# Sinkhorn attention and a token-mixing MLP on one core: a rewritten second half of the hand-written order, wider weights for turning k', and a last output row in two halves

## The chip, the cores and the metric

The kernel runs on one core of a Trainium2 chip. The time is device microseconds of one execution; the figure quoted is the median of several runs. One of the executions was also recorded by the hardware profiler, and all rows below come from that recording.

## What is computed

Four batches, eight heads, 768 positions, head size 64. The reference first turns an 8 by 8 matrix per head into a nearly doubly stochastic P by five rounds of exp and normalisation, mixes the eight blocks of 96 positions of k and v with it, attends within each block, and passes the result x (768 by 512 per batch) through a mixer over positions:

```python
k_sorted = np.einsum('bhij,bhjcd->bhicd', P, k_b)        # v_sorted likewise
scores = scale * np.matmul(q_b, k_sb.transpose(0, 1, 2, 4, 3))
attn = exp(scores - max) / sum;  x = attn @ v_sb
wq = x @ w_q;  wk = x @ w_k
mixed = (wq @ wk.T / 8) @ x
out = np.maximum(mixed, 0.0) @ w_out
```

The first half is written per head, the mixer per batch. The kernel computes mixed as wq times (wk.T x), so that no 768 by 768 matrix is made.

## The kernel before

All work is cut into units with short names, and one string, `ORDER` (from line 20), lists them in program order; line 661 walks through it. A unit's name is a letter, the batch and a number: `P23` is product group 3 of batch 2. Capital letters are TensorE units that write PSUM, and the number behind the colon is the first of the 512-column PSUM banks (0 to 7) that they write; the same letter in lower case is the unit that empties the banks, with its engine (A ScalarE, D VectorE, G GpSimd, S SyncE). A TensorE unit therefore waits until whoever used its banks last has emptied them. Each engine works through its own units in the order of the string, so the string decides both the sequence on every engine and which unit waits for which.

The units, batch by batch (a batch has `b`, the line is that of the function):

- `l`: loads of q, k, v by GpSimd's queue (line 220); `p`, `Q`/`q`: q is rearranged by a copy and turned by TensorE (262, 271, 274), two heads at a time.
- `K`/`k` and `V`/`v`: sorted k (turned, two heads at a time, 289) and sorted v (310); `R`: six DMAs per batch that bring sorted v from `Vs` into blocks, `VT` (329). `K`, `V`, `S`, `P`, `H` write two banks.
- `S`/`e`: seven groups of scores, emptied by ScalarE with exp into `E` (352, 361).
- `P`/`r`, `x`: five groups of products with v; VectorE takes the reciprocal of the sums and multiplies, into `X` (372, 385, 389). Group 4 is the small one.
- `T`/`t` (batches 0 and 1, TensorE) or `D` (batches 2 and 3, two transposing DMAs on SyncE's queue, 397): `X` is turned into `XT`. `D20` needs product groups 0 to 2 of batch 2, `D21` groups 2 to 4.
- `J`/`j`: wq and wk of one half of the positions each, turned, into `qkT` (408); `d` copies the wq part to the other 64 partitions, `qD`. `J` needs all of `XT`, so both transposing DMAs.
- `W`/`w`: wk (the change calls it k') is turned back by TensorE with `qkT` as the weights (423). `G`/`g`: wk.T x, into `Ab` (433). `H`/`h`: mixed, turned, with relu, into `mixT` (448, 456), three units per batch, each for two of the six output rows that a partition holds.
- `O`/`o`: output row n of a batch, four matmuls of 512 columns, copied to one of four buffers `ot` (469, 478). Two rows share a buffer; `s` sends them out by the queue of the engine named (482). For the last batch each row is sent by itself. A number of two digits behind the batch, as in `O323`, means a half row (`osplit`): half 2 of row 3.
- `Z`: dummy matmuls at the start, while the inputs arrive.

The buffer of rows n, n+1 of batch b is number (3b + n/2) modulo 4, so rows 2 and 3 of batch 2 (sent by `s21`) lie in the buffer that rows 4 and 5 of batch 3 (`o34`, `o35`) take over. Behind the last unit GpSimd checks all reciprocals (`guard`) and, if one isn't finite, recomputes everything in another way; with these inputs it does not.

The loop that walks the string:

```python
    for item in ORDER.split():
        kind, arg = item[0], item.split(":")[1:]
        ...
        if kind.isupper() and kind not in "RNDI":
            fns[kind](b, n, int(arg[0]))
        else:
            fns[kind](b, n, arg[0], int(arg[1]) if len(arg) > 1 else None)
```

Of the kernel before, what the change touches and what calls it, by code (L numbers as in the profile page):

```python
# [19 lines left out]
ORDER = """  # L20
i00:G i02:D I00:S A00:0 Z04:1 Z15:1 Z25:1 lv0b I01:S lk0a c00:D a01:A i03:G c01:D lv0a a02:A:0 lk0b
c02:D z11:A lv1b lv1a a03:A Q01:0 Z33:1 c03:D lk1a lq1b lk1b z10:A a04:A c04:D z12:A Q00:2 Z43:1
q01:D:0 a05:A z13:A c05:D q00:A:2 Z54:1 Q03:0 Z62:1 q03:D:0 B00:2 Q02:3 n01:D:2 n00:D:2 n03:D:2
u00:A:2 K01:4 K00:0 q02:D:3 n11:G n10:G k01:A:4 Y03:6 k00:D:0 y03:A:6 S02:4 n02:D:2 e02:A:4 Y00:0
K02:2 Y02:6 y00:A:0 k02:D:2 Y01:4 y02:A:6 S00:0 y01:D:4 lp K03:2 e00:A:0 S01:6 k03:D:2 F00:4 lq1a
e01:A:6 F01:5 f00:D:4 S06:2 S05:0 e06:A:2 f01:D:5 P00:6 e05:A:0 S03:2 r00:D:6 x00:D:6 V12:4 e03:A:2
P01:0 r01:D:0 x01:D:0 v12:A:4 S04:6 F03:2 F02:3 e04:A:6 R15:S V11:4 f02:D:3 V10:0 v11:A:4 f03:D:2
P02:6 p12:G v10:A:0 r02:D:6 x02:D:6 R12:S p13:G P04:2 R14:S K11:4 n20:G T00:0 r04:D:2 x04:D:2
k11:A:4 R13:S Q12:1 P03:6 R11:S t00:A:0 q12:D:1 lk2a K13:2 r03:D:6 x03:D:6 R10:S Q13:1 k13:A:2 lv2b
K12:4 U00:0 k12:A:4 lv2a K10:2 z01:D:0 T03:6 q13:D:1 k10:A:2 T02:7 t03:D:6 U01:4 p11:G T01:5 t02:D:7  # L30
z02:A:4 S16:2 S14:0 t01:D:5 lo e16:A:2 S15:6 Q11:4 e15:A:6 p10:G J01:5 q11:D:4 J00:2 e14:A:0 n21:G
S13:6 j00:D:2 j01:A:5 Q10:0 e13:A:6 W01:1 lq2a W00:1 P14:2 P13:4 w00:A:1 d01:G r14:D:2 x14:D:2
q10:A:0 K20:6 lq2b G00:1 r13:D:4 x13:D:4 k20:A:6 lq3a S11:2 G01:1 e11:A:2 d00:G K21:6 g00:D:1 S10:4
lk2b k21:D:6 H01:0 e10:A:4 h01:D:0 V20:2 V21:4 v20:A:2 V22:6 v21:D:4 P10:0 v22:A:6 R21:S T13:2
r10:D:0 x10:D:0 R20:S H02:4 S12:6 O02:3 R25:S e12:A:6 h02:D:4 R23:S H00:0 o02:A:3 P12:6 R22:S
h00:A:0 O03:3 p21:G r12:D:6 x12:D:6 R24:S t13:A:2 P11:4 lk3a O04:0 r11:D:4 x11:D:4 p20:G O00:2
o04:A:0 lv3a p23:A T10:0 o00:D:2 lv3b Q21:1 p22:A Q20:4 q21:D:1 T11:2 n31:G q20:A:4 T12:5 t11:D:2
O05:1 t12:A:5 o03:D:3 lq3b t10:D:0 S22:6 S20:4 e22:A:6 S21:2 lk3b o05:D:1 J11:0 p30:G e21:A:2 Q23:1
j11:D:0 J10:6 p31:G q23:D:1 e20:A:4 Q22:7 j10:D:6 W11:1 n30:G Q30:0 q22:A:7 K22:4 q30:D:0 K23:2
k22:A:4 Q31:0 s01:G k23:D:2 W10:1 P21:6 d10:G w10:A:1 d11:D S23:4 q31:D:0 S24:2 e23:A:4 O01:1  # L40
r21:D:6 x21:D:6 e24:A:2 S25:4 G10:0 o01:D:1 e25:A:4 K31:6 K30:2 k31:D:6 G11:0 k30:A:2 P22:4 g10:D:0
S26:2 r22:D:4 x22:D:4 V30:0 e26:A:2 P23:6 v30:A:0 H10:2 r23:D:6 x23:D:6 V31:4 h10:A:2 R30:S p33:G
S31:0 R31:S v31:D:4 e31:A:0 p32:G V32:6 H12:2 v32:A:6 S32:0 h12:D:2 R33:S Q33:4 Q32:5 e32:A:0 R32:S
K32:6 q33:D:4 R34:S P24:2 k32:A:6 K33:0 r24:D:2 x24:D:2 R35:S k33:A:0 P20:6 q32:D:5 D21:S H11:2
S35:0 r20:D:6 x20:D:6 h11:A:2 O14:5 e35:A:0 S33:2 o14:D:5 D20:S S36:6 O13:4 e33:A:2 P31:0 s00:S
e36:A:6 S34:2 r31:D:0 x31:D:0 P34:6 e34:A:2 O10:5 r34:D:6 x34:D:6 P32:2 o10:A:5 S30:0 r32:D:2
x32:D:2 P33:6 e30:A:0 J20:5 J21:0 r33:D:6 x33:D:6 j20:A:5 P30:2 d20:G j21:A:0 W20:5 r30:D:2 x30:D:2
d21:G W21:5 D31:S O12:6 w20:A:5 G21:5 o13:D:4 D30:S G20:5 o12:D:6 O11:4 g20:D:5 s11:S H20:6 s02:S
H22:2 h20:A:6 H21:0 h22:D:2 O15:5 o11:A:4 O21:6 o15:D:5 h21:A:0 s10:G O20:7 J30:0 J31:1 j30:D:0
O25:5 d30:G j31:D:1 d31:S W30:4 o20:D:7 W31:4 O22:1 w30:A:4 w31:A:4 o25:D:5 o21:A:6 G31:0 s12:A  # L50
G30:0 s20:A O23:6 o22:A:1 g30:A:0 H30:0 o23:D:6 H31:4 h30:A:0 H32:2 h31:D:4 O24:7 s21:S h32:A:2
O31:6 o24:A:7 O32:2 o31:D:6 s22:S O34:3 s31:A o32:D:2 O35:6 s32:A o34:A:3 O30:7 o35:D:6 s34:S O33:3
s35:A o30:D:7 s30:S o33:A:3 s33:S
"""


# [652 lines left out]
```

## Time and profile before

| | |
|---|---|
| median of 3 runs | 98.72 us (98.5 to 98.78) |
| the profiled execution's own time | 98.33 us |
| its span in the profile | 96.4 us |
| busy: TensorE / weight loads | 86.3 us (90%) / 58.7 us (61%) |
| busy: VectorE / ScalarE / GpSimd | 72.6 / 68.8 / 43.1 us |
| granted clock of TensorE | 0.991 of full speed over the span |
| DMA | 21.44 MB, 222 GB/s over the span |

The span runs from the first to the last recorded event; the execution's own time is 1.93 us longer. Busy times are sums over instructions, so an engine that is 90% busy over the span can be idle in one stretch and never idle in another; a busy TensorE need not be at its peak, because matmuls overlap and their ends are modelled. In the rows, PE is TensorE, PEld its weight loads, DVE VectorE, ACT ScalarE, POOL GpSimd and SP SyncE. "<-" at the end of a row names what ended the idle time before it.

### The profile page before, as it was taken

The numbers are of one execution on the slowest core, as the hardware profiler recorded it, in microseconds if no ns is written. First come the engines' busy times: TensorE is split into PE (matmuls) and PEld (weight loads), VectorE is DVE, ScalarE is ACT, GpSimd is POOL, SyncE is SP. The second block draws the span as 40 slices with busy tenths as digits, with TensorE's granted clock in tenths as the row PEclk, the third lists the DMA queues.
The fourth block names the chain that finished last, engine by engine and source line by source line (L and its number), as shares of the span: only waits on it lengthen the run. The fifth ranks groups of instructions, "written<-read, shape, count | busy, mean of one in ns | idle before, by whom it ended". The sixth has DMA issues, their size and how long they took to land.

```text
span 96.4 us, 3206 instructions
## 1 busy us (share of the span) xinstructions
PE 86.3 (90%) x1333; PEld 58.7 (61%) x1342; DVE 72.6 (75%) x141; ACT 68.8 (71%) x96; POOL 43.1 (45%) x70
## 2 busy tenths in 40 slices
PE   4999587999899999999999999899969999999930
PEld 2344177788787687845778687674756545644400
DVE  2767896988999469999877999987796773645520
ACT  5177629998979999796989888999746090466220
POOL 6996309700999993049998006000004021950000
PEclk9999999999999999999999999999999999999996
DMA  0899999999999999999999999379953899785992
GB/s 10 266 353 227 203 203 203 203 203 207 195 275 216 209 203 207 202 204 249 250 225 204 202 204 289 124 208 206 205 206 70 199 118 413 289 352 221 396 366 112
DMA packets 24655, 21.44 MB, mean 222 GB/s; under 512 B 7296, under 2 KB 22720, under 8 KB 24640
## 3 DMA queue, kind: packets, MB, share of 16 engines
q0 software_dynamic: 12720, 10.36, 65.5%
q1 hardware_dynamic: 11200, 9.05, 35.5%
q10 hardware_dynamic: 720, 1.84, 4.8%
q8 instruction: 10, 0.16, 0.7%
q14 instruction: 5, 0.04, 0.1%
HBM read 20.19 MB, written 6.29 MB: 275 GB/s over the span
## 4 chain that ended last, share of the span: by engine, by line
PE 55%; DVE 16%; ACT 12%; DMA 10%; issue 3%; SPq 0%; DVEq 0%; ACTq 0%
PE ps L154 55%; DMA XT<-X 5%; DMA XT<-in_q_dram 5%; DVE X L392 4%; ACT E L363 4%; ACT KT L158 3%; DVE QT L162 2%; ACT Vs L158 2%; DVE VT L162 1%; DVE Vs L162 1%; DVE M L253 1%; DVE XT L162 1%; ACT mixT L460 1%; ACT Qn L158 1%; DVE tmp L193 1%
## 5 line engine op out<-in xcount | busy, mean ns | idle before, releaser
L363 ACT ACTIVATE E<-ps 96x960 bf16<-96x960 f32 (+1 forms) x28 | 24.3, 905 | 2.2 <-PE ps L154 1.6
L154 PE MATMUL ps<-wo,mixT 128*128 128x512 bf16 x88 | 22.8, 380 | 0.4
L392 DVE TENSOR_TENSOR X<-ps,Rall 96x896 bf16<-96x896 f32 (+1 forms) x20 | 20.1, 1006 | 0.7
L160 POOL COPY Qn<-Qn 128x768 bf16<-128x768 bf16 x10 | 8.1, 831 | 16.9 <-DMA Qn<-in_q_dram 16.9
L162 DVE COPY ot<-ps 128x512 f32<-128x512 f32 (+1 forms) x16 | 10.8, 687 | 4.8 <-PE ps L154 4.5
L154 PEld LDWEIGHTS <-mixT 128*128 128x128 bf16 x96 | 8.3, 98 | 9.1 <-issue 0.8
L154 PE MATMUL ps<-VT,E 96*128 96x65 bf16 x256 | 11.2, 193 | 0.3
L154 PEld LDWEIGHTS <-KT 64*128 64x128 bf16 (+1 forms) x288 | 8.4, 97 | 4.5 <-issue 2.2
L154 PEld LDWEIGHTS <-E 96*128 96x128 bf16 x256 | 9.7, 97 | 2.1 <-issue 0.4
L158 ACT CAST KT<-ps 128x768 bf16<-128x768 f32 x13 | 10.2, 808 | 0.9 <-DVE Rall L387 0.4
L154 PE MATMUL ps<-QT,KT 64*128 64x96 bf16 x256 | 9.3, 204 | 1.1 <-ACT KT L158 0.8
L160 POOL COPY qD<-qkT 64x384 bf16<-64x384 bf16 x6 | 3.0, 505 | 15.0 <-ACT qkT L158 12.8
L460 ACT ACTIVATE mixT<-ps 128x1024 bf16<-128x1024 f32 x7 | 7.1, 1027 | 3.5 <-PE ps L154 3.5
L253 POOL TENSOR_TENSOR M<-PTR,m_p 128x512 bf16<-128x512 bf16 x6 | 7.9, 1318 | 3.6 <-ACT PTR L158 3.5
L158 ACT COPY ot<-ps 128x512 f32<-128x512 f32 x9 | 5.3, 587 | 5.1 <-PE ps L154 4.7
L154 PE MATMUL ps<-idb,Qn 128*128 128x128 bf16 x96 | 7.7, 220 | 1.1 <-DVE Pm L190 1.0
L154 PE MATMUL ps<-fil 128*128 128x512 bf16 x25 | 8.2, 482 | 0.1
L154 PE MATMUL ps<-M,Kn 128*64 128x128 bf16 x192 | 7.8, 221 | 0.1
L162 DVE CAST KT<-ps 128x768 bf16<-128x768 f32 x7 | 6.7, 955 | 1.2 <-PE ps L154 1.1
L154 PEld LDWEIGHTS <-Qn 128*128 128x128 bf16 x96 | 5.7, 98 | 3.0 <-ACT Qn L158 2.1
L158 ACT CAST Vs<-ps 128x1024 bf16<-128x1024 f32 x7 | 7.0, 1012 | 0.6 <-PE ps L154 0.5
L387 DVE RECIPROCAL Rall<-ps 96x14 f32<-96x14 f32 (+1 forms) x20 | 4.6, 228 | 3.5 <-PE ps L154 2.2
(84 smaller groups left out, 142.9 us busy)
## 6 DMA issues: line engine op xcount, KB each, us to landing
Vn<-in_v_dram POOLq DMA_DIRECT2D x8, 384.0 KB, 9.6
Kn<-in_k_dram POOLq DMA_DIRECT2D x8, 384.0 KB, 11.4
out_dram<-ot SPq DMA_DIRECT2D x5, 512.0 KB, 4.7
VT<-Vs SPq DMA_DIRECT2D x18, 132.0 KB, 5.0
Qn<-in_q_dram POOLq DMA_DIRECT2D x6, 384.0 KB, 11.4
XT<-in_q_dram SPq DMA_DIRECT2D x2, 768.0 KB, 5.7
out_dram<-ot POOLq DMA_DIRECT2D x2, 512.0 KB, 7.4
out_dram<-ot ACTq DMA_DIRECT2D x2, 512.0 KB, 2.8
```

The lines of the kernel that those rows point to most:

```text
L154: nc.tensor.matmul(o, w, x, is_transpose=t, start=start, stop=stop, skip_group_check=True)
L158: nc.scalar.copy(o, i)
L160: nc.gpsimd.tensor_copy(o, i)
L162: nc.vector.tensor_copy(o, i)
L193: nc.vector.reduce_sum(tmp, (Pm if n == 1 else Pv).rearrange("p i j -> p j i"), axis=AX.X)
L253: ENG[e].tensor_tensor(out=M[b % 2][:, h0:h0 + hn], in0=src.unsqueeze(2).to_broadcast([P, hn, SP, NB]), in1=m_p.unsqueeze(1).unsqueeze(3). ...
L363: nc.scalar.activation(E[b % 2][:, n, 0:2 * w * BLK].rearrange("p (t a c) -> p a t c", a=2, c=BLK), PS[0:BLK, bank:bank + 2, 0:w * BLK].re ...
L387: nc.vector.reciprocal(Rall[:, b, n, :, 0:w], avps(bank, w)[:, :, :, D])
L392: nc.vector.tensor_mul(xo.rearrange("p (a t d) -> p a t d", a=2, d=D), avps(bank, w)[:, :, :, 0:D], Rall[:, b, n, :, 0:w].unsqueeze(3).to_ ...
L460: nc.scalar.activation(o, i, ACT.Relu)
```

## The change

From the loads of the last batch on, the units stand in another order: from about 48 us of the span to its end. What was done before by the other engine of the pair is marked by the letter. Of the units that empty banks or copy, `j10`, `d11`, `k31`, `g10`, `h12`, `d20`, `o13`, `h22`, `j30`, `o23`, `o35` go to ScalarE, and `q22`, `w10`, `k33`, `h10`, `o11`, `h21`, `d31`, `w30`, `o21`, `o22`, `o24` to VectorE; `d30` goes to SyncE. Of the output DMAs `s01`, `s22`, `s34` go to ScalarE's queue, `s12`, `s32`, `s35` to SyncE's, `s20` and `s21` to GpSimd's. Row 3 of the last batch is computed, copied and sent in two halves of 256 columns. In the first half of the string TensorE, ScalarE and VectorE keep their sequences, but many units use other banks, so that some wait for another unit to empty theirs: `S13` now follows `S14` in its banks and no longer `S15`.

The end of the table, and the one function that changes:

```diff
-O31:6 o24:A:7 O32:2 o31:D:6 s22:S O34:3 s31:A o32:D:2 O35:6 s32:A o34:A:3 O30:7 o35:D:6 s34:S O33:3
-s35:A o30:D:7 s30:S o33:A:3 s33:S
+O31:2 o24:D:3 O30:0 s22:A o31:D:2 O32:1 s31:A o30:D:0 O35:2 s30:S o32:D:1 O34:3 s32:S o35:A:2 s35:S
+O323:2 o34:A:3 O313:1 o323:D:2 s34:A o313:D:1 s323:A s313:A
```
```diff
     def u_W(b, n, bank):
         for i in range(4 * n, 4 * n + 4):
-            mm(PS[0:BLK, bank, i * DH:(i + 1) * DH], qkT[b % 2][:, i * BLK:(i + 1) * BLK], idb[:, DH:P])
+            w = BLK if i % 4 == 3 else P
+            mm(PS[0:w, bank, i * DH:(i + 1) * DH], qkT[b % 2][:, i * BLK:i * BLK + w], idb[:, DH:P])
```

So three of four weight loads of `W` take 128 columns (the block's 96 and 32 of the next), and 128 rows of PSUM are written, of which 96 are read; in the fourth they stay 96.

On TensorE, between the units that both versions share, the order from the last `W` of batch 1 to the first `J` of batch 2 is, before:

```
W11 Q30 K22 K23 Q31 W10 P21 S23 S24 O01 S25 G10 K31 K30 G11 P22 S26 V30 P23 H10 V31 S31 V32 H12 S32
Q33 Q32 K32 P24 K33 P20 H11 S35 O14 S33 S36 O13 P31 S34 P34 O10 P32 S30 P33 J20 J21
```

and now:

```
W11 K23 K22 W10 Q30 Q31 S25 S24 O01 P20 S23 G11 K31 G10 P21 S26 V30 V31 V32 P24 H11 P22 K30 H12 P23
S31 Q33 Q32 K32 K33 S32 O14 S36 S35 H10 S34 O15 P34 S33 P33 O10 P32 S30 P31 J21 J20
```

Both hold the same kinds and numbers of units (`O15` for `O13`, `P31` for `P33` before the `J`).

The first place where instructions move is VectorE's row of units around the products of batch 2 (`X0`; `Rall` takes the reciprocals, `Vs0` is sorted v of batch 3, `QT1` and `KT1` are its q and k, `mixT1` the mixer of batch 1). Before, from the reciprocals of `P22` on:

```order
L387 RECIPROCAL Rall_109<-ps_66 96x14
L392 TENSOR_TENSOR X0_89<-ps_66,Rall_109 96x896
L387 RECIPROCAL Rall_109<-ps_66 96x14
L392 TENSOR_TENSOR X0_89<-ps_66,Rall_109 96x896
L162 CAST Vs0_84<-ps_66 128x8x2x64
L462 TENSOR_SCALAR mixT1_102<-ps_66 128x4x256
L162 COPY QT1_81<-ps_66 128x768
L387 RECIPROCAL Rall_109<-ps_66 96x2x4
L392 TENSOR_TENSOR X0_89<-ps_66,Rall_109 96x512
L162 COPY QT1_81<-ps_66 128x768
L387 RECIPROCAL Rall_109<-ps_66 96x14
L392 TENSOR_TENSOR X0_89<-ps_66,Rall_109 96x896
```

Now, from the eviction of `V31` on:

```order
L162 CAST Vs0_84<-ps_66 128x8x2x64
L387 RECIPROCAL Rall_109<-ps_66 96x2x4
L392 TENSOR_TENSOR X0_89<-ps_66,Rall_109 96x512
L387 RECIPROCAL Rall_109<-ps_66 96x14
L392 TENSOR_TENSOR X0_89<-ps_66,Rall_109 96x896
L387 RECIPROCAL Rall_109<-ps_66 96x14
L392 TENSOR_TENSOR X0_89<-ps_66,Rall_109 96x896
L162 COPY QT1_81<-ps_66 128x768
L162 CAST KT1_83<-ps_66 128x768
L162 COPY QT1_81<-ps_66 128x768
L463 TENSOR_SCALAR mixT1_102<-ps_66 128x4x256
```

The last three product groups of batch 2 (groups 4, 2, 3) now follow one another, and both copies of q and one of k of batch 3 stand behind them instead of between and before.

The second place is the end of ScalarE's row, from the copy of a row of the last batch on (`ot` are the output buffers). Before:

```order
L158 COPY ot0_103<-ps_66 128x512
L488 DMA out_0_dram<-ot1_104 128x512
L488 DMA out_0_dram<-ot2_105 128x512
L158 COPY ot3_106<-ps_66 128x512
L488 DMA out_0_dram<-ot3_106 128x512
L158 COPY ot2_105<-ps_66 128x512
```

Now:

```order
L486 DMA out_0_dram<-ot0_103 128x1024
L489 DMA out_0_dram<-ot1_104 128x512
L158 COPY ot3_106<-ps_66 128x512 x2
L489 DMA out_0_dram<-ot3_106 128x512
L489 DMA out_0_dram<-ot2_105 128x256 x2
```

The last copy of a whole row has left ScalarE, and its queue ends with three DMAs, of rows 4 and of the two halves of row 3; the halves are copied by VectorE, as its last two copies.

The third place is GpSimd's row between the copies of q of batch 3 (`Qn2`) and its check of the reciprocals (`s1`). Before:

```order
L160 COPY Qn2_71<-Qn1_70 128x2x6x64 x2
L160 COPY qD0_95<-qkT0_93 64x384 x2
L485 DMA out_0_dram<-ot3_106 128x1024
L160 COPY qD1_96<-qkT1_94 64x384
L500 TENSOR_REDUCE s1_1795<-Rall_109 1x1
```

Now:

```order
L160 COPY qD0_95<-qkT0_93 64x384
L486 DMA out_0_dram<-ot3_106 128x1024
L486 DMA out_0_dram<-ot2_105 128x1024
L486 DMA out_0_dram<-ot3_106 128x1024
L501 TENSOR_REDUCE s1_1801<-Rall_109 1x1
```

Two copies for batches 2 and 3 have left GpSimd, and two output DMAs of batch 2, `s20` and `s21`, have come to it; the check stands behind them.

## Rows read from the trace of the kernel before

**Rows 1.** Busy time by stretch; columns: stretch, length, engines with instructions, clock, DMA.
```profile
core 0: us, PE busy (x) PEld busy (x) DVE busy (x) ACT busy (x) POOL busy (x), PEclk, DMA share, GB/s
51.26:71.57 20.31, 18.99 (x382) 14.12 (x383) 17.84 (x30) 18.00 (x23) 3.00 (x5) 1.00 1.09 203
71.57:92.50 20.93, 20.77 (x159) 10.82 (x162) 12.92 (x19) 8.97 (x15) 5.29 (x11) 1.00 0.83 264
```

**Rows 2.** Chain that ended last, in order of time: start, length, what (us).
```profile
66.33 5.19 DMA XT<-X
...
92.54 0.59 ACT ot L158
```

**Rows 3.** Timeline, TensorE: start, us, instructions merged, and the idle time before them.
```profile
60.54 0.61 PE L154 MATMUL ps<-Vn,M 128*128 128x128 bf16 x8 [0.35 <-DVE X L392]
...
61.45 0.39 PE L154 MATMUL ps<-QT,KT 64*128 64x96 bf16 x10
...
61.77 0.84 PE L154 MATMUL ps<-idb,Qn 128*128 128x128 bf16 x12
...
62.54 0.53 PE L154 MATMUL ps<-M,Kn 128*64 128x128 bf16 x12
...
63.00 0.42 PE L154 MATMUL ps<-VT,E 96*128 96x65 bf16 x8
...
71.57 1.47 PE L154 MATMUL ps<-XT,wqk 128*128 128x384 bf16 x8 [0.68 <-DMA XT<-X]
...
85.53 0.28 PE L154 MATMUL ps<-qkT,Ab 64*128 64x256 bf16 x1
...
86.29 6.22 PE L154 MATMUL ps<-wo,mixT 128*128 128x512 bf16 x27
```

**Rows 4.** Groups of instructions by form: busy us, mean ns of one, idle before.
```profile
L363 ACT ACTIVATE E<-ps 96x960 bf16<-96x960 f32 x24 | 22.5, 974 | 1.9 <-PE ps L154 1.3 <-DVE XT L162 0.2 <-DVE X L392 0.2
L392 DVE TENSOR_TENSOR X<-ps,Rall 96x896 bf16<-96x896 f32 x16 | 17.4, 1087 | 0.6
...
L162 DVE COPY ot<-ps 128x512 f32<-128x512 f32 x15 | 10.1, 686 | 4.8 <-PE ps L154 4.5 <-DMA out_dram<-ot 0.2
L154 PEld LDWEIGHTS <-E 96*128 96x128 bf16 x256 | 9.7, 97 | 2.1 <-issue 0.4 <-ACT E L363 0.2
...
L158 ACT COPY ot<-ps 128x512 f32<-128x512 f32 x9 | 5.3, 587 | 5.1 <-PE ps L154 4.7 <-ACT ot L158 0.5
...
L387 DVE RECIPROCAL Rall<-ps 96x14 f32<-96x14 f32 x16 | 3.8, 236 | 2.6 <-PE ps L154 1.3 <-ACT E L363 1.2
...
L162 DVE CAST Vs<-ps 128x1024 bf16<-128x1024 f32 x2 | 2.4, 1213 | 0.0
...
L154 PEld LDWEIGHTS <-qkT 128*96 128x96 bf16 x32 | 2.0, 124 | 0.3
...
L446 DVE TENSOR_SCALAR Ab<-ps 128x256 bf16<-128x256 f32 x3 | 1.3, 417 | 0.1
```

**Rows 5.** Timeline, DMA issues on the queues of SyncE and ScalarE: start, us, issue.
```profile
64.58 1.65 SPq L398 DMA_TRANSPOSE XT<-X  x1
...
66.33 1.57 SPq L398 DMA_TRANSPOSE XT<-X  x1
...
91.54 0.34 ACTq L488 DMA_DIRECT2D out_dram<-ot  x1
```

**Rows 6.** DMA issues of single short windows: size, then median us from issue to landing.
```profile
Qn<-in_q_dram POOLq DMA_DIRECT2D x1, 384.0 KB, 11.4
...
out_dram<-ot POOLq DMA_DIRECT2D x1, 512.0 KB, 10.1
...
out_dram<-ot POOLq DMA_DIRECT2D x1, 512.0 KB, 4.6
...
qD<-qkT SPq DMA_DIRECT2D x1, 48.0 KB, 1.8
...
out_dram<-ot SPq DMA_DIRECT2D x1, 256.0 KB, 2.2
```

More of the change, by code (lines that the diff above doesn't have):

```diff
@@ L20 @@
 ORDER = """
[L21 to L49, printed above, removed]
@@ L50 @@
-O25:5 d30:G j31:D:1 d31:S W30:4 o20:D:7 W31:4 O22:1 w30:A:4 w31:A:4 o25:D:5 o21:A:6 G31:0 s12:A
-G30:0 s20:A O23:6 o22:A:1 g30:A:0 H30:0 o23:D:6 H31:4 h30:A:0 H32:2 h31:D:4 O24:7 s21:S h32:A:2
-O31:6 o24:A:7 O32:2 o31:D:6 s22:S O34:3 s31:A o32:D:2 O35:6 s32:A o34:A:3 O30:7 o35:D:6 s34:S O33:3
-s35:A o30:D:7 s30:S o33:A:3 s33:S
+i00:G i02:D I00:S lv0b A00:0 I01:S Z04:1 lk0a c00:D a01:A i03:G c01:D Z15:2 lv0a a02:A:0 lk0b c02:D
+lv1b z11:A Z25:0 lv1a a03:A c03:D lk1a z10:A Q01:2 lq1b Z33:3 a04:A c04:D Q00:0 Z43:3 z12:A lk1b
@@ new lines @@
+q01:D:2 a05:A z13:A Z54:1 c05:D q00:A:0 Q03:2 Z62:3 q03:D:2 B00:3 Q02:0 n01:D:3 n00:D:3 K01:4
+n03:D:3 K00:6 q02:D:0 u00:A:3 k01:A:4 n11:G k00:D:6 Y03:0 y03:A:0 S02:4 n02:D:3 Y00:6 n10:G K02:2
+e02:A:4 Y02:0 k02:D:2 y00:A:6 Y01:4 lp S00:2 y01:D:4 y02:A:0 K03:6 e00:A:2 lq1a k03:D:6 S01:0 F00:4
+e01:A:0 F01:5 f00:D:4 S06:6 S05:2 f01:D:5 e06:A:6 P00:0 e05:A:2 S03:6 r00:D:0 x00:D:0 V12:4 e03:A:6
+P01:2 r01:D:2 x01:D:2 v12:A:4 S04:0 F03:6 F02:7 e04:A:0 R15:S V11:4 f02:D:7 V10:2 v11:A:4 p12:G
+f03:D:6 P02:0 p13:G P04:6 v10:A:2 r02:D:0 x02:D:0 R12:S K11:4 n20:G R14:S k11:A:4 T00:2 r04:D:6
@@ new lines @@
+x04:D:6 R13:S Q12:3 t00:A:2 P03:4 lk2a R11:S q12:D:3 K13:6 r03:D:4 x03:D:4 R10:S Q13:3 lv2b k13:A:6
+K12:0 U00:2 lv2a k12:A:0 K10:6 z01:D:2 T03:4 q13:D:3 k10:A:6 T02:5 p11:G t03:D:4 U01:0 T01:1 t02:D:5
+z02:A:0 S16:6 lo S14:2 t01:D:1 e16:A:6 S15:4 e15:A:4 p10:G Q11:0 J01:1 q11:D:0 n21:G e14:A:2 J00:4
+j01:A:1 S13:2 j00:D:4 lq2a Q10:1 e13:A:2 W01:0 W00:0 d01:G P14:4 P13:6 w00:A:0 r14:D:4 x14:D:4 lq2b
+K20:2 q10:A:1 G00:0 lq3a r13:D:6 x13:D:6 k20:A:2 S11:4 d00:G G01:0 e11:A:4 K21:2 lk2b g00:D:0 S10:6
@@ new lines @@
+k21:D:2 H01:0 e10:A:6 V20:4 h01:D:0 V21:2 v20:A:4 V22:6 v21:D:2 v22:A:6 P10:0 R21:S T13:4 R20:S
+r10:D:0 x10:D:0 H02:6 S12:2 R25:S O02:5 e12:A:2 R23:S h02:D:6 H00:0 o02:A:5 R22:S P12:2 p21:G
+h00:A:0 O03:5 R24:S r12:D:2 x12:D:2 lk3a t13:A:4 P11:6 O04:0 p20:G r11:D:6 x11:D:6 O00:4 lv3a
+o04:A:0 p23:A lv3b T10:0 o00:D:4 Q21:1 p22:A Q20:6 n31:G q21:D:1 T11:4 q20:A:6 T12:7 t11:D:4 O05:1
+t12:A:7 o03:D:5 lq3b t10:D:0 S22:2 lk3b S20:6 e22:A:2 S21:4 o05:D:1 J11:0 p30:G e21:A:4 Q23:1
+j11:D:0 J10:2 n30:G q23:D:1 e20:A:6 Q22:3 W11:1 q22:D:3 K23:4 p31:G j10:A:2 K22:6 k23:D:4 W10:1
@@ new lines @@
+k22:A:6 Q30:0 d10:G Q31:2 q30:D:0 d11:A S25:4 S24:6 w10:D:1 s01:A O01:3 e25:A:4 q31:D:2 P20:0
+e24:A:6 S23:4 r20:D:0 x20:D:0 G11:2 e23:A:4 K31:6 G10:2 o01:D:3 k31:A:6 P21:4 g10:A:2 S26:0 r21:D:4
+x21:D:4 V30:6 e26:A:0 V31:2 v30:A:6 V32:0 v31:D:2 P24:4 v32:A:0 R31:S H11:6 r24:D:4 x24:D:4 R30:S
+P22:2 h11:A:6 R33:S K30:0 p33:G r22:D:2 x22:D:2 H12:4 k30:A:0 R35:S P23:6 p32:G h12:A:4 R32:S S31:0
+r23:D:6 x23:D:6 Q33:2 R34:S Q32:3 e31:A:0 K32:4 D20:S q33:D:2 K33:6 k32:A:4 S32:0 k33:D:6 O14:2
+e32:A:0 D21:S q32:D:3 S36:6 S35:4 e36:A:6 H10:0 e35:A:4 s00:S h10:D:0 S34:6 s02:S O15:3 e34:A:6
@@ new lines @@
+o14:D:2 P34:0 S33:4 r34:D:0 x34:D:0 P33:6 e33:A:4 O10:2 r33:D:6 x33:D:6 P32:4 o10:A:2 S30:0 r32:D:4
+x32:D:4 P31:6 e30:A:0 J21:2 r31:D:6 x31:D:6 J20:0 D31:S j21:A:2 P30:4 d21:G j20:A:0 W21:2 r30:D:4
+x30:D:4 W20:2 O11:0 w20:A:2 d20:A G20:2 o15:D:3 D30:S G21:2 o11:D:0 O12:3 g20:D:2 s10:G H20:0
+o12:D:3 H21:4 h20:A:0 H22:6 h21:D:4 O13:2 O21:3 o13:A:2 h22:A:6 s11:S O20:2 o21:D:3 s12:S J31:4
+o20:D:2 J30:5 j31:D:4 s20:G O22:2 d31:D j30:A:5 d30:S W31:3 W30:3 O23:5 w31:A:3 w30:D:3 o22:D:2
+G31:4 G30:4 O25:2 g30:A:4 o23:A:5 H30:6 s21:G o25:D:2 H31:4 h30:A:6 H32:0 h31:D:4 O24:3 h32:A:0
```

## The prediction, made blind

> **What bounds the kernel now.** I read four views in turn. First the busy time by stretch [rows 1], cut where TensorE ends `W11` (51.26 us), where it starts `J20` (71.57), and where its last matmul ends (92.50). The reader is to see two kinds of stretch. From 71.57 on TensorE is busy for 20.77 of 20.93 us: nothing but its own work sets the time. From 51.26 to 71.57 it is busy for 18.99 of 20.31, so 1.32 us are idle, while ScalarE (18.00) and VectorE (17.84) are nearly as full as TensorE: here three engines hold each other up. The granted clock is full in both, so no term below is about the clock. Next the chain that ended last [rows 2]: it passes through a transposing DMA of 5.19 us, issued at 66.33, and ends in ScalarE's copy of the last output row, 0.59 us. Then TensorE's timeline [rows 3], for the places of the idle time: `J20` starts 0.68 us late, waiting for that DMA, and `V32` 0.35 us late, waiting for VectorE's product `x23`. These two are 1.03 of the 1.32 us. The views of prices and DMAs [rows 4 to 6] are used below.
>
> So the change can gain in the middle stretch, at most 1.32 us unless it shortens TensorE's work, and behind the last matmul; from `J` on only by fewer nanoseconds per matmul.
>
> **The wait for the transposing DMAs.** Before, the last product group of batch 2 ahead of its transposing DMAs is `P20`; between it and `J20` TensorE has thirteen units. In the new order it is `P23`, and the same kinds of thirteen units stand behind it plus six: `S31`, `Q33`, `Q32`, `K32`, `K33`, `S32`. A group of scores takes 61.77 - 61.45 = 0.32 us, the two `Q` 62.54 - 61.77 = 0.77, a `K` 63.00 - 62.54 = 0.46 [rows 3], so the six take 2 x 0.32 + 0.77 + 2 x 0.46 = 2.33 us. Against it: before, the two DMAs were issued 66.33 - 64.58 = 1.75 us apart and the first, `D21`, was out long before `x20` ended [rows 5]. Now `x22` and `x23` follow each other on VectorE, 0.236 + 1.087 = 1.32 us apart [rows 4], while SyncE needs 1.65 us to issue a transposing DMA [rows 5]; the second goes out 0.33 us later than its data allow. The DMA is covered by 2.33 - 0.33 - 0.68 = 1.32 us more than it needs. The wait goes, **-0.68 us**, as long as the six `R` transfers, ahead of `D20` on SyncE's queue, are out by then; they follow `V30`, `V31`, `V32`, which now stand together and ahead of `P24`, so I expect them earlier than before. If that cover is gone, each microsecond by which the `R` are late is one that `J21` is late.
>
> **What is late next.** ScalarE and VectorE swap units in this stretch. By kinds the exchange is nearly even (`j10`, `k31`, `g10`, `h12` against `q22`, `k33`, `w10`, `h10`; besides, ScalarE takes a small copy and one DMA issue of 0.34 us [rows 5]). So ScalarE holds some 18.3 us and VectorE 17.8 in a stretch that would be 19.6 us without the wait: there is room, but little. The 0.35 us of `V32` go too: its banks now follow `e26`, which is short and early. A new wait comes: `P22` takes the banks of `V31`, whose eviction (1.21 us) stands on VectorE behind `x21` (0.24 + 1.09) [rows 4], so TensorE stands at `P22` for a few tenths. I put it at 0.33, about one wait like `V32`'s. Ends for the whole stretch: 0, where every wait comes back in another place, and -1.32, where TensorE never stands. Sum: -0.68 - 0.35 + 0.33 = **-0.70 us**.
>
> **The first half.** `S13` has the banks of `S14` and no longer those of `S15`. Since `e14` is ScalarE's next eviction after `e15`, `S13` may wait up to one eviction longer, 0.97 us [rows 4]; ends 0 and +0.97. TensorE has had two units between, and the units that follow wait less for ScalarE, so I take the value nearer to nothing: **+0.10**.
>
> **Weights of 128 columns.** A load of 96 columns takes 124 ns, one of 128 columns 97 [rows 4]. So 27 ns per load is the most that can come out of it, and nothing the least, as loads overlap matmuls; I take half, 13 ns. Of the 24 changed loads 12 lie behind `J21`, where TensorE is the bound: 12 x 13 ns = **-0.15 us**; the others lie beside evictions and count nothing (if TensorE were the bound there too, as much again). The Trainium skill (TensorE: Matmul & The Clock Gate, section "LDWEIGHTS (loading the stationary operand)") speaks against this edit: a load takes its columns divided by 1.2 in nanoseconds, 80 for 96 columns and 107 for 128. By that rule the term would be +0.3 and the sum below -0.65. The rows above show the wider load as the quicker one, so here the measurement decides; the same page's section on Fast Weight Load, by which 128 weights of two bytes take a faster path, agrees with them.
>
> **The end.** The last copy was 0.587 us for 512 columns on ScalarE; now it is 256 columns on VectorE: between half of 0.686 and the 0.417 of `Ab` of that size [rows 4], 0.39, so -0.20. The last transfer had 256 KB and landed in 2.2 us; one of 48 KB took 1.8 [rows 6]; for 128 KB I take 1.95, between, so -0.25. On ScalarE's queue the last DMA stands behind two more issues of 0.34 [rows 5]: `o34` ends 0.6 us after `O34`, then two issues, 1.28; the second half's copy ends 0.9 (a row's matmuls) + 0.4 = 1.3 after `O34`. So the queue costs 0.05 at most. Eight matmuls of 256 columns instead of four of 512 cost four more weight loads beside them: 0 to 4 x 0.097; I take 0.05. Sum **-0.35** (ends -0.6 and 0).
>
> **Edits that I cost at nothing.** `d30` by SyncE takes 1.8 us [rows 6] instead of a copy, but lies beside `O22`, `W`, `O23`, `G` and `O25`, some 4 us; without that cover it would cost about 1.3. `d11` and `d20` on ScalarE lie beside `G`. On SyncE's queue `s02` stands ahead of `D31`, and `s11` and `s12` ahead of `d30`; all wait for rows copied by then. GpSimd's check starts behind `s21`, yet GpSimd is busy for only 5.29 us of the last 20.93 [rows 1] and stays clear of the end.
>
> **The sum.** -0.70 + 0.10 - 0.15 - 0.35 = **-1.10 us**. The profiled execution took 98.33 us, which becomes 97.23. It lies 0.39 below the median of the runs; I take the difference over to the median: 98.72 - 1.10 = **97.62**, say 97.6 us.
>
> **Rivals.**
>
> - *The evictions are the bound.* If ScalarE and VectorE, not the DMA, hold the middle stretch, the waits come back in front of other units and only the end is gained: 0 + 0.10 - 0.15 - 0.35 = -0.40, **98.3 us**. For it: 18.00 and 17.84 of 20.31 us. Against it: both still have 2.3 us of idle time there.
> - *The last loads come late.* `s01`, 512 KB, was queued on GpSimd's queue behind the loads of batch 3 and so took 10.1 us [rows 6]. On ScalarE's queue it competes with them. At 203 GB/s [rows 1] it pushes them back by at most 2.6 us; q's last load then lands up to 14 us after its issue instead of 11.4 [rows 6], and `Q33` and `K32` stand. Most of that is slack (`Q33` ran some 3 us after that load landed); I give it 0.6 us: **98.2 us**.
> - *`s21` by GpSimd comes too late.* `o35` overwrites the buffer that `s21` reads. `s21` is issued behind `o23`, about when `H30` starts; `o35` follows three `H` (86.29 - 85.53 = 0.76) and five rows of 6.22 / 7 = 0.89 [rows 3], 5.2 us later. On GpSimd's queue such a transfer took 4.6 us in one place and 10.1 in another [rows 6]. Beyond 5.2 us each microsecond is added at the end; beyond 6.3 the change is slower. At 10.1 it would be -1.10 + 4.9 = +3.8, **102.5 us**. Against it: the 10.1 lay behind loads, and here there are none.
> - *The middle stretch loses all its idle time* (-1.32) and the end gives its best (-0.6): with the other terms -2.0, **96.7 us**.
>
> **How the numbers follow.** The forecast, from -0.5 to -1.6 us, has a chance of 0.58; the evictions 0.15, the loads 0.08, `s21` 0.07, the best case 0.12. A difference of 0.3% is 0.30 us, about what a measurement of this kernel can tell from none. Faster by more than that are the forecast, the best case, and the larger part of the two small gains: 0.80. Within it falls the rest of those two: 0.12. Slower: `s21`, and a little for the first half at its dear end: 0.08. The range reaches from the best case to the small gains and a little beyond: 96.7 to 98.6; outside lie `s21` and the tails.
>
> **What would show it.** Right: `J21` starts within a tenth of `P31`'s end and no wait for XT<-X stands before it; it begins near 70.9 us; from it to the last matmul some 20.8 us; the last copy takes 0.4, its transfer 1.9 to 2.0. Wrong: idle time of TensorE in front of `P22`, `K33` or `P34` that adds up to a microsecond; a wait of a copy of q for its load near 60 us; a copy into `ot` waiting for out_dram<-ot near 89 us; or a first half in which `W11` ends later than 51.5 us.

## The result, and the profile after

The changed kernel took 99.36 us (median; 99.12 to 100.04), the kernel before, run beside it, 98.44. The ratio is 1.0109, with a 95% interval of 1.0075 to 1.0143: **1.1% slower**. It leaves out one slow run of the kernel before, of 99.93 us, which the median includes. The forecast was 97.6 us and faster, the range ended at 98.6, and slower had a chance of 0.08. The profiled execution took 99.33 us, its span 97.5 (98.33 and 96.4 before).

The same views as before, cut at the same units: end of `W11`, start of the first `J`, last matmul. First the busy time by stretch of the changed kernel.

```profile
core 0: us, PE busy (x) PEld busy (x) DVE busy (x) ACT busy (x) POOL busy (x), PEclk, DMA share, GB/s
51.31:70.39 19.08, 18.24 (x379) 14.03 (x381) 17.08 (x28) 17.26 (x24) 2.34 (x4) 1.00 1.10 201
70.39:91.70 21.31, 21.00 (x169) 10.94 (x168) 14.82 (x24) 10.04 (x16) 5.44 (x11) 1.00 0.89 276
91.70:97.50 5.80, 0.00 (x0) 0.00 (x0) 0.39 (x2) 0.00 (x0) 0.00 (x0) 0.75 0.33 120
```

Beside [rows 1]: `W11` ends at 51.31 us (51.26 before), the middle stretch lasts 19.08 us (20.31), and the last matmul ends at 91.70 (92.50). TensorE is done 0.80 us *earlier*, and the span ends 1.1 us *later*. So all of the loss, 1.9 us, lies behind the last matmul: that piece was 3.9 us (92.50 to 96.4) and is 5.8 now, and the engines' columns show almost nothing in it. Next VectorE's last copies, ScalarE's last three DMA issues, and the third of them by itself.

```profile
91.30 0.79 DVE L162 COPY ot<-ps 128x256 f32<-128x256 f32 x2 [1.56 <-PE ps L154]
91.39 1.45 ACTq L489 DMA_DIRECT2D out_dram<-ot  x3
92.43 0.42 ACTq L489 DMA_DIRECT2D out_dram<-ot  x1
```

```profile
out_dram<-ot ACTq DMA_DIRECT2D x2, 128.0 KB, 2.1
```

The last output transfer (third row of the first fence: the issue; the second fence is the median time to landing of the two halves, of which the last took 2.0) went out at 92.43 us and landed at 94.4. Before, the last issue began near 93.15 and landed 2.2 us later, at 95.4, a microsecond ahead of the end of the span [rows 6]. The output is complete 0.9 us sooner than before, and the program still ends 1.1 us later. What ends last isn't the output. In the changed kernel the chain that ended last stops at VectorE's copy:

```profile
81.01 5.20 PE ps L154 x49
86.26 4.95 PE ps L154 x24
91.30 0.79 DVE ot L162 x2
```

That is 92.09 us, and 5.4 us of the span stand behind it without a link. The waits of SyncE's queue put a name on its last stand, and a wrong one:

```profile
SPq L705 <- DMA Vn<-in_v_dram: 3.4, 1, 3.4
SPq L705 <- PEq L705: 2.4, 2, 1.9
```

(Columns: the waiting line, what released it, us in total, times, longest. L705 is the end of the program.) A load of v, landed some 40 us earlier, can't have been what SyncE waited for. In the kernel before the same stand reads so:

```profile
SPq L704 <- DMA out_dram<-ot: 1.3, 3, 0.6
```

What does end last shows among the instructions that don't count as busy. Here is GpSimd in the changed kernel, from its last output DMA on, with the first and last of the seven instructions of `guard`, the check of the reciprocals; then, by line, its instructions at the branch (L676) and at the program's end (L705: count, shortest, median and longest in ns, first and last start in us).

```profile
84.92 0.53 POOL L486 DMA_DIRECT2D out_dram<-ot  x1 [4.09 <-ACT ot L158]
85.51 0.76 POOL L501 CROSS_LANE_REDUCE s<-Rall 96x1 f32<-96x280 f32 x1
...
89.05 0.18 POOL L507 TENSOR_SCALAR flag<-s 1x1 int32<-1x1 f32 x1
```

```profile
L676 POOLq EVENT_SEMAPHORE  x5: 17/43/43, 93.2 to 93.5; - x5
L676 POOLq COMPARE_BRANCH  x1: 45/45/45, 90.0 to 90.0; - x1
L676 POOLq INC_SWDGE_SEM  x1: 756/756/756, 93.6 to 93.6; - x1
L705 POOLq EVENT_SEMAPHORE  x4: 17/17/17, 96.8 to 97.4; - x4
L705 POOLq DRAIN  x3: 46/101/2355, 94.4 to 97.3; - x3
```

And the same of the kernel before:

```profile
82.24 0.76 POOL L500 CROSS_LANE_REDUCE s<-Rall 96x1 f32<-96x280 f32 x1
...
85.78 0.18 POOL L506 TENSOR_SCALAR flag<-s 1x1 int32<-1x1 f32 x1
```

```profile
L675 POOLq COMPARE_BRANCH  x1: 45/45/45, 86.6 to 86.6; - x1
L675 POOLq INC_SWDGE_SEM  x1: 736/736/736, 90.6 to 90.6; - x1
L704 POOLq DRAIN  x3: 46/101/2273, 91.4 to 96.1; - x3
```

Follow the times in the changed kernel: check 85.51 to 89.23, branch at 90.0, next instruction at 93.2, `INC_SWDGE_SEM` 93.6 to 94.4, `DRAIN` 94.4 to 96.75, the meeting of the engines, end of the span at 97.5. If nothing in this chain waits for another engine before that meeting, the check's start alone sets its end; from there to the end of the span it takes **12.0 us**. Before, the check started at 82.24 and the long `DRAIN` ended at 91.4 + 2.27 = 93.7. With the 0.75 us that follow it in the changed kernel the chain alone would have ended at 94.4, and the output's last landing set the end, at 96.4: 2.0 us of slack. Now the check starts behind `s21` on GpSimd's queue. `s21` waits for the copy of its row (4.09 us of standing, `<-ACT ot`), and the check starts at 85.51, 3.27 us later. 3.27 - 2.0 = 1.3 us would be the loss if the chain kept its length; it became 0.2 us shorter (from the check's start to the `DRAIN`'s end 11.2 us, 11.4 before), and the spans differ by 1.1. This is only a sum within two traces, and it needs tests from outside.

That was the theory that the experiments had to test. Its rivals: `s21` itself, by landing late or by holding a buffer; the 128-column weights; the halves; and the order of units from the loads on.

### The profile page after: what moved, and what is told of

The parts are those of the page before. It is cut to its first block, busy times and chain, and to the rows that moved or that the text cites. A ratio compares the mean times of both kernels' runs of the same rounds, so it can differ in the third digit from the quotient of the medians.

```text
span 97.5 us, 3216 instructions
## 1 busy us (share of the span) xinstructions
PE 86.1 (88%) x1337; PEld 58.9 (60%) x1346; DVE 73.8 (76%) x144; ACT 68.5 (70%) x96; POOL 42.7 (44%) x69
## 4 chain that ended last, share of the span: by engine, by line
PE 64%; DVE 14%; ACT 7%; DMA 5%; issue 4%; SPq 0%; DVEq 0%; ACTq 0%
PE ps L154 64%; DMA XT<-in_q_dram 5%; ACT Vs L158 2%; ACT E L363 2%; DVE QT L162 1%; DVE VT L162 1%; DVE Vs L162 1%; DVE X L392 1%; DVE XT L162 1%; DVE KT L162 1%; DVE M L253 1%; DVE ot L162 1%; ACT Qn L158 1%; DVE tmp L193 1%; ACT KT L158 1%
## 5 line engine op out<-in xcount | busy, mean ns | idle before, releaser
L154 PE MATMUL ps<-wo,mixT 128*128 128x512 bf16 (+1 forms) x92 | 22.5, 370 | 0.5 <-issue 0.2
L162 DVE COPY ot<-ps 128x512 f32<-128x512 f32 (+2 forms) x19 | 12.4, 658 | 5.3 <-PE ps L154 5.1
L160 POOL COPY Qn<-Qn 128x768 bf16<-128x768 bf16 x10 | 8.2, 829 | 18.4 <-DMA Qn<-in_q_dram 12.6
L162 DVE COPY QT<-ps 128x768 bf16<-128x768 bf16 x13 | 7.1, 545 | 0.9 <-PE ps L154 0.9
L158 ACT COPY ot<-ps 128x512 f32<-128x512 f32 x7 | 4.1, 585 | 4.8 <-PE ps L154 4.8
L160 POOL COPY qD<-qkT 64x384 bf16<-64x384 bf16 x4 | 2.0, 508 | 11.1 <-ACT qkT L158 11.0
```

The source lines that it names most:

```text
L158: nc.scalar.copy(o, i)
L160: nc.gpsimd.tensor_copy(o, i)
L162: nc.vector.tensor_copy(o, i)
```

## The experiments

All ratios are to the kernel before, run beside them, with 95% intervals. The first four ran on one chip, the fifth to eighth on another, the last four on a third; the kernel before took 98.30, 98.11 and 97.99 us there.

**1. `s20` and `s21` onto SyncE** (on the changed kernel; in the kernel before `s20` was on ScalarE's queue and `s21` on SyncE's), so that the check follows `s10`. Of the string only the items that change are shown.

```diff
- s20:G
+ s20:S
- s21:G
+ s21:S
```

> The changed kernel with s20 and s21 sent by SyncE's queue instead of GpSimd's. Theory (GpSimd's check of the reciprocals, pushed behind s21, ends the kernel: 12.0 us from its first instruction at 85.51 to the span's end at 97.5): the check now starts behind s10, near 76 us, ends its chain near 88, and the span ends 1.0 us after the last output transfer lands, near 95.5 us; time near 97.4 us, 1% below the kernel before. Rival (the output transfers themselves, or the lower clock at the end, make the tail longer): the span stays near 97.5, time near 99.4 us.

Measured: 97.51 us, ratio 0.9918 (0.9895 to 0.9940). The check started at 76.30:

```profile
76.30 0.75 POOL L501 CROSS_LANE_REDUCE s<-Rall 96x1 f32<-96x280 f32 x1
```

Two letters take away 1.9% and turn the change into a gain: the place of these two DMAs is the whole loss.

**2. The same two DMAs onto GpSimd in the kernel before**, with nothing else of the change.

```diff
- s20:A
+ s20:G
- s21:S
+ s21:G
```

> The kernel before with nothing changed but s20 and s21, which go to GpSimd's queue. Theory: the check starts behind s21, which waits for o23 (copied until about 86.3 us), so near 86.9 instead of 82.24; 12.0 us from there is 98.9, 2.5 us behind the old end: about 100.9 us against 98.4. Rival (the place of these two DMAs doesn't matter): 98.4 us.

Measured: 101.16 us, ratio 1.0284 (1.0256 to 1.0312), span 99.2. The check and what follows it:

```profile
87.28 0.76 POOL L500 CROSS_LANE_REDUCE s<-Rall 96x1 f32<-96x280 f32 x1
```

```profile
L675 POOLq COMPARE_BRANCH  x1: 45/45/45, 91.7 to 91.7; - x1
L704 POOLq DRAIN  x3: 46/101/2437, 95.9 to 98.9; - x3
```

The check starts 87.28 - 82.24 = 5.04 us later than before; minus the slack of 2.0 that is 3.0 us, and the span is 99.2 - 96.4 = 2.8 us longer. From the check to the end it is 11.9 us, where 12.0 had been expected. The loss comes without the new order, and within 0.2 us of the size that the chain gives.

**3. `s21` alone back on SyncE** (`s20` stays on GpSimd).

```diff
- s21:G
+ s21:S
```

> The changed kernel with s21 alone moved to SyncE's queue; s20 stays on GpSimd's. Theory: the check starts behind s20, near 80.9 us, and its chain ends near 92.9, ahead of the output: the same as with both moved, about 97.4 us. Rival (any late transfer on GpSimd's queue has to be drained at the end): between 98.4 and 99.4 us.

Measured: 97.21 us, ratio 0.9894 (0.9867 to 0.9920). The check started at 81.00:

```profile
81.00 0.76 POOL L501 CROSS_LANE_REDUCE s<-Rall 96x1 f32<-96x280 f32 x1
```

With 12.0 us the chain ends at 93.0, 2.3 us ahead of the span's end at 95.3. One DMA decides, and with the chain clear of the end it doesn't matter that it starts 4.7 us later than in experiment 1.

**4. The check early, both DMAs left on GpSimd.** Its seven instructions are issued ahead of `s20`; only the reading of the flag and the branch stay behind `s21`.

```diff
-    def guard():
+    def guard_flag():
...
-        return g.value_load(flag[0:1, 0:1])
+        return flag
...
+        if name == "s20":
+            flag = guard_flag()
...
-    off = guard()
+    off = nc.gpsimd.value_load(flag[0:1, 0:1])
```

> The changed kernel with both DMAs left on GpSimd's queue, but the check's seven instructions placed ahead of s20; only the reading of its flag and the branch stay behind s21. Theory: the flag is read when s21 is issued, near 85.5 us; from the flag's end to the span's end the changed kernel took 97.5 - 89.2 = 8.3 us, so the chain ends near 93.8, ahead of the output (95.5): about 97.4 us. Rival (the two transfers on GpSimd's queue, not the check behind them, hold the end): 99.4 us.

Measured: 96.91 us, ratio 0.9872 (0.9847 to 0.9897). GpSimd and, by line, its end:

```profile
79.59 0.18 POOL L507 TENSOR_SCALAR flag<-s 1x1 int32<-1x1 f32 x1
...
84.75 0.54 POOL L486 DMA_DIRECT2D out_dram<-ot  x1 [3.82 <-ACT ot L158]
```

```profile
L678 POOLq COMPARE_BRANCH  x1: 45/45/45, 85.3 to 85.3; - x1
L678 POOLq EVENT_SEMAPHORE  x5: 17/43/43, 89.0 to 89.3; - x5
L707 POOLq DRAIN  x3: 46/101/2355, 90.2 to 94.8; - x3
```

`s21` is issued from the same queue at the same time as in the changed kernel (84.75 and 84.92), so the transfer and its queue are innocent: it is the check behind it. The branch now comes at 85.3 instead of 90.0, the long `DRAIN` ends at 92.5, and the end is the output's again. This is the lowest ratio of the study, together with its repeat (9) and variant (12), though the intervals of 3 and 5 overlap it.

**5. No recomputation behind the branch.** The body that recomputes everything if a reciprocal isn't finite is left out and replaced by one small memset; the place of `s20`, `s21` and the check is that of the change.

```diff
-        general(nc.gpsimd, gp, dram)
+        nc.gpsimd.memset(gp.tile([1, 2], FP32, name="none"), 0.0)
```

> The changed kernel as it was, check behind s21, but the recomputation that GpSimd jumps over (some 9460 instructions) is left out and a memset of two numbers stands in its place; the recomputation doesn't run with these inputs. Theory 1 (the 3.2 us between GpSimd's branch at 90.0 and its next semaphore at 93.2 are the price of the far jump): the chain ends some 3 us earlier, near 94.5, the output at 95.5 sets the end, and the time is near 97.4 us. Theory 2 (the 3.2 us are the price of any branch, or of the transfers that GpSimd still has under way): the span stays near 97.5 and the time near 99.3 us.

Measured: 97.10 us, ratio 0.9898 (0.9860 to 0.9936).

```profile
L676 POOLq COMPARE_BRANCH  x1: 45/45/45, 90.3 to 90.3; - x1
L676 POOLq EVENT_SEMAPHORE  x1: 17/17/17, 90.5 to 90.5; - x1
L705 POOLq DRAIN  x3: 46/101/2355, 90.6 to 95.2; - x3
```

The branch is as late as in the changed kernel (90.3, there 90.0), yet the loss is gone: the next instruction comes 0.2 us behind it instead of 3.2, there is no `INC_SWDGE_SEM`, and the `DRAIN`, 2.36 us as ever, ends at 93.0. So 3.0 + 0.8 us of the chain are the price of the body that is never run: the jump over it, and an `INC_SWDGE_SEM` that stands there only with it.

With the check out of the way, 6 to 12 ask what the rest of the change is worth. They build on kernel 4, except 10.

**6. `W` at 96 columns**, and **7. row 3 of the last batch in one piece**, each alone undone on kernel 4.

```diff
-            w = BLK if i % 4 == 3 else P
+            w = BLK
```

> The kernel with the check early (96.9 us), and all weight loads of W back at 96 columns. Theory: 12 loads of 13 ns behind J21 come back, 0.15 us: 97.05 us; W of batch 3 takes about 0.34 us from start to the next unit instead of 0.26. Rival (wider loads do nothing for the time, as loads overlap matmuls): 96.9 us.

```diff
-O323:2 o34:A:3 O313:1 o323:D:2 s34:A o313:D:1 s323:A s313:A
+O33:2 o34:A:3 o33:D:2 s34:A s33:A
```

> The kernel with the check early (96.9 us), and row 3 of the last batch in one piece: O33, copied by VectorE, sent by ScalarE's queue behind s34. Theory: the last copy is 0.69 instead of 0.42 us, the last transfer 256 KB instead of 128 (2.3 against 2.1 us), but one DMA issue of 0.34 us less stands ahead of it, so that a part comes back: 0.2 to 0.4 us more, 97.1 to 97.3 us. Rival (halves only add issues and weight loads): 96.9 us or less.

Measured: 6 97.42 us, ratio 0.9936 (0.9915 to 0.9957); 7 97.28 us, ratio 0.9920 (0.9892 to 0.9949). Kernel 4 and its repeat stand at 0.9872 and 0.9881, on the two other chips. By these ratios the wide weights would be worth 0.6%, the halves 0.4%. The interval of 6 lies apart from kernel 4's and from its repeat's, that of 7 overlaps both. But both comparisons go from chip to chip, and experiments 8 and 12 below show what that can be worth: one and the same kernel, which can't be told from kernel 4, has 0.9911 on the chip of 6 and 7 and 0.9872 on the third. Against its 0.9911 the weights would be worth 0.25%, the halves 0.1%, and the intervals overlap. TensorE's timeline shows less of the weights: batch 3's `W`, first in kernel 6, then in the changed kernel, lasts from the start of its row to that of the next.

```profile
81.75 0.51 PE L154 MATMUL ps<-idb,qkT 128*96 128x64 bf16 x8
82.09 1.03 PE L154 MATMUL ps<-wo,mixT 128*128 128x512 bf16 x4
```

```profile
81.44 0.43 PE L154 MATMUL ps<-idb,qkT 128*128 128x64 bf16 x8
81.70 1.03 PE L154 MATMUL ps<-wo,mixT 128*128 128x512 bf16 x4
```

0.34 and 0.26 us: 0.08 less for six changed loads, 13 ns each. The rest of kernel 6's half a microsecond isn't in these loads. In its profile it is there before the first `J`, which starts at 70.99 us, in kernel 4's and its repeat's at 70.55 and 70.51; but in experiment 11's profile, with the same 96-column `W`, it starts at 70.58. So the profiles don't tie this delay to the weights.

For the halves, first the end of kernel 7, then of the repeat of kernel 4:

```profile
91.79 0.69 DVE L162 COPY ot<-ps 128x512 f32<-128x512 f32 x1 [1.91 <-PE ps L154]
92.52 0.34 ACTq L489 DMA_DIRECT2D out_dram<-ot  x1
```

```profile
91.35 0.79 DVE L162 COPY ot<-ps 128x256 f32<-128x256 f32 x2 [1.56 <-PE ps L154]
92.48 0.41 ACTq L489 DMA_DIRECT2D out_dram<-ot  x1
```

The copies end at 92.48 with the whole row and at 92.14 with the halves, but the last issue starts at 92.52 and 92.48: three issues in a row on ScalarE's queue give back nearly all that the shorter copy gains. What is left is the landing, 1.8 us for the last half and 2.0 for the row.

**8 and 12. `s34` on SyncE** (on kernel 4), so that only two issues stand on ScalarE's queue at the end.

```diff
-o323:D:2 s34:A 
+o323:D:2 s34:S 
```

> The kernel with the check early (96.9 us), and s34 on SyncE's queue instead of ScalarE's. Theory: the last DMA, s313, no longer stands behind two issues; it was issued near 92.3 us though its half was copied at about 91.9, so the end comes 0.2 to 0.3 us earlier: 96.65 us. Rival (the landing, or the bandwidth of the last transfers, sets the end): 96.9 us.

> The kernel with the check early and s34 on SyncE's queue once more, beside the one with s34 on ScalarE's queue on the same chip. If the issues ahead of s313 cost time, this one is 0.2 to 0.3 us faster; if the landing sets the end, the two are equal.

Measured: 97.05 us, ratio 0.9911 (0.9884 to 0.9937), and again, beside kernel 4: 96.85 us, ratio 0.9872 (0.9837 to 0.9906). Kernel 4 beside it (9) stood at 0.9881. No difference can be told. The profiles say why: in 8 the last issue starts at 92.22 us, in 9 at 92.48, but the transfer takes 2.1 and 1.8 us to land, so that the output is complete at 94.3 in both.

**9. Kernel 4 once more**, beside 10 to 12.

> The kernel with the check early once more, as the measure for the next three on their chip: it had a ratio of 0.9872 to the kernel before. Expected 0.985 to 0.991.

Measured: 96.97 us, ratio 0.9881 (0.9851 to 0.9912): the gain of 1.2 to 1.3% holds on another chip.

**10. `W` with 128 columns alone in the kernel before.** The edit is the diff of 6 the other way round.

> The kernel before with nothing changed but the 128-column weight loads of W. Theory: 24 loads at 10 to 13 ns, of which those behind J20 and in front of TensorE-bound work count: 0.1 to 0.3 us less, ratio 0.997 to 0.999. Rival (the wider loads carry most of the gain that the order seemed to bring): 0.7 us less or more, ratio 0.993 or less.

Measured: 97.94 us, ratio 0.9988 (0.9963 to 1.0013): between a gain of 0.37% and a loss of 0.13%. Inconclusive, and not in favour of the half a microsecond that 6 seemed to show.

**11. The order alone**: kernel 4 with both edits of 6 and 7.

> The new order alone: the kernel with the check early, with weight loads of W at 96 columns and the last output row in one piece. Theory (the order carries the middle stretch, where J21 starts 1.0 to 1.2 us earlier): about 0.8 to 0.9 us less than before, ratio 0.991 to 0.992; W and the halves make up the rest to 0.987. Rival (the order brings little without them): ratio 0.996 or more.

Measured: 97.45 us, ratio 0.9949 (0.9925 to 0.9973), a gain of 0.26 to 0.73 us, between the two values that were expected. Kernel 9 beside it is better by 0.68 points, and the intervals don't overlap: weights and halves together are worth some 0.67 us (0.48 by the medians, 97.45 and 96.97), and the order, with the new places of its DMAs, some 0.5. How the first part divides between weights and halves stays open.

## Why the prediction was wrong, point by point

**The step that failed** is the sentence "GpSimd's check starts behind `s21`, yet GpSimd is busy for only 5.29 us of the last 20.93 and stays clear of the end". It reads a busy time where a chain had to be followed. GpSimd was idle, but its idle time was a wait in order: `s21` stands until its row is copied, and the check stands behind it. And the check is not the engine's end: branch, jump, `INC_SWDGE_SEM` and `DRAIN` follow, 8.3 us behind the flag (97.5 - 89.23), none of it counted as busy. The rows were there in the trace of before: flag ready at 85.96, the long `DRAIN` ending at 91.4 + 2.27 = 93.7 in a span of 96.4. `s21` on GpSimd could have been placed at `o23`'s end, about when `H30` starts, as the rival on `s21` does: 85.53 [rows 3]. 85.53 + 0.6 for the issue + 11.4 from the check's start to the `DRAIN`'s end gives 97.5, for a span that was 96.4. The warning was one addition away. Experiments 1 to 5 show this cause: moved alone, each way, it brings the loss and takes it away.

**The wait for the transposing DMAs and the middle stretch: right in sign, too small.** -0.70 us was forecast, -1.23 came (20.31 to 19.08). Idle time fell from 1.32 to 0.84 us, and busy time from 18.99 to 18.24: "at most 1.32 us unless it shortens TensorE's work" took busy time for work. Short stands between matmuls are merged into a row of the timeline and count as busy: `K32` and `K33` together took 62.90 to 63.76 = 0.86 us in the changed kernel, 0.46 + 0.61 before. The Trainium skill (Perfetto Trace Analysis, section "Identifying the Most-Contended Engine") says that the busy share of matmuls is no good measure of how close a kernel is to what TensorE can do, because pipelined instructions look smaller in a trace than they are. Here the busy time misled the other way: in a stretch of 20 us 0.75 us of it went without any unit going.

**The new wait at `P22`: right.** Forecast 0.33, measured 0.40, at the place and with the cause named:

```profile
59.86 0.59 PE L154 MATMUL ps<-VT,E 96*128 96x65 bf16 x14 [0.40 <-DVE Vs L162]
70.39 1.64 PE L154 MATMUL ps<-XT,wqk 128*128 128x384 bf16 x8
71.87 0.60 PE L154 MATMUL ps<-VT,E 96*128 96x65 bf16 x14
```

**The cover of the DMA: thinner than forecast.** No wait stands ahead of the first `J` (second row), but its eight matmuls last 1.64 us, 1.48 to the next unit, where 1.31 is a `J` without a stand. SyncE's queue shows why:

```profile
59.03 4.67 SPq L330 DMA_DIRECT2D VT<-Vs  x6
...
65.45 1.64 SPq L398 DMA_TRANSPOSE XT<-X  x1
```

The six `R` issues hold the queue from 59.03 to 63.70, so `D20` goes out at 63.80 and `D21` at 65.45; the second landed 5.4 us later, at 70.85, when the first `J` had begun. "1.32 us more than it needs" was all used up: about 0.2 us of wait was left (1.48 - 1.31), and 0.31 in experiment 5, where two matmuls went ahead and six waited, as the first two read only what `D20` brings:

```profile
71.33 1.14 PE L154 MATMUL ps<-XT,wqk 128*128 128x384 bf16 x6 [0.31 <-DMA XT<-X]
```

The prediction had named the condition, the `R` transfers out by then, and took it for met: they were out 0.8 us sooner than before (63.70 and 64.48), which wasn't enough to keep that cover.

**The first half: right.** `W11` ends 0.05 us later, 0.10 was forecast.

**The weights: the price per load right, the term open.** 13 ns per load of `W`'s time, as taken (the loads themselves went from 124 to 99 ns). What they do to the whole isn't settled: 0.5 to 0.6% by experiment 6 against kernel 4 on other chips, 0.25% against experiment 8 on its own, -0.37 to +0.13% by experiment 10, with the start of the first `J` moving between 70.4 and 71.0 us from kernel to kernel. On the rule of the Trainium skill by which a load takes its columns divided by 1.2 (TensorE: Matmul & The Clock Gate, section "LDWEIGHTS (loading the stationary operand)") the wide `W` would be the dearer one; `W`'s 0.26 against 0.34 us says the opposite.

**From the first `J` to the last matmul: 0.5 us too short.** 20.8 us were forecast, 21.31 came (20.93 before): about 0.2 is the late second transfer above, 0.2 is `W20`, which waits for `j20`'s eviction (the chain goes through it at 72.13, 0.49 us, to 72.66; both `W` take 0.71 us, 0.49 before), and 0.1 the halves' four extra weight loads, for which 0.05 was taken. The stretch before had gained 0.5 more than forecast, so the last matmul came out 0.80 us earlier, with 0.70 to 0.75 forecast.

**The end: parts right, sum too good.** The copy took 0.79 / 2 = 0.40 (0.39 forecast), the landing 2.0 (1.95). But the queue's price was not 0.05 at most: three issues took 1.45 us, and the last began 0.34 us after its copy had ended. Measured against the last matmul the landing came only some 0.1 us sooner, instead of 0.35.

**Rivals.** "The last loads come late" happened and cost nothing: q's last load landed 12.6 us after its issue (11.4 before), the copies of q waited for it until 59.86 (58.73 before), and `Q33`, at 62.13, didn't stand. That `s01` pushed it back, as the rival has it, wasn't tried alone.

```profile
59.86 1.59 POOL L160 COPY Qn<-Qn 128x768 bf16<-128x768 bf16 x2 [7.39 <-DMA Qn<-in_q_dram]
```

"`s21` by GpSimd comes too late" had the right instruction and the wrong victim: the transfer landed in 2.9 us, and `o35`'s copy waited for its matmuls alone. What decided stood behind it on the queue. With that repaired the change gives 1.2 to 1.3% (experiments 4, 9), about the 1.1 us that was forecast. That it comes so near is in part luck: the middle stretch gave 0.5 us more, and what lies behind it 0.5 and 0.25 us less.

## What to carry to other kernels

Before moving a waiting instruction to an idle engine, list what is queued behind it there up to the end of the program, and add up their durations, the uncounted ones too: an engine that is busy for a quarter of a stretch can still be the one that ends last. A branch over a large body that is never run has a price at the end of the kernel; compute its condition as soon as its inputs are final, ahead of anything that waits. If the span goes on after the last landing, and the waits name a transfer that landed long ago, read each engine's control instructions line by line.

## What the runs showed that was not expected

- The jump over the body that isn't run: 3.2 us from the branch to GpSimd's next instruction in the changed kernel, 3.6 before, 3.7 in kernel 4, and between 3.0 (experiment 2) and 3.8 (experiment 1) wherever the body stands; 0.2 with the body replaced by one instruction. What takes this time inside wasn't tried.
- GpSimd's last long `DRAIN` took 2.20 to 2.44 us in all profiles, with or without that body. The Trainium skill (VectorE: DVE Perf Modes, section "The DRAIN you can't avoid") puts the `DRAIN`s that are added at a kernel's start and end at about 12 ns on all five engines; SyncE's agree (7 to 13 ns), GpSimd's doesn't, and the measurement decides. TensorE's and VectorE's longest (1.06 and 0.46 us in the changed kernel) end about with their last matmul and copy; GpSimd's begins 5 us behind its last counted instruction. Its length follows the number of DMAs that GpSimd has issued in the whole kernel: 26 DMAs 2.20 us (experiment 1), 27 DMAs 2.27 (before), 28 DMAs 2.36 (changed), 29 DMAs 2.44 (experiment 2), so some 0.08 us for each one moved there; `INC_SWDGE_SEM` grows beside it by about 0.02 (0.72, 0.74, 0.76, 0.78). What it does in that time no run shows.

```profile
L705 SPq DRAIN  x3: 7/7/13, 94.9 to 97.0; - x3
```

- The last wait of SyncE was put down to a load of v (3.4 us; 2.6 in experiment 2) in the two kernels where GpSimd's end was the last, and to the output's landing in every other.
